# First group's x prepared during the last attention pair, decoded weights copied by ScalarE, x items spread over each group

## The chip, the cores and the metric

One core of a Trainium2 chip runs the whole program. The metric is the device time of one execution in microseconds (us). Engines: PE is TensorE's matmul, PEld its weight load, DVE VectorE, ACT ScalarE, POOL GpSimd, SP SyncE, which issues nearly all the DMAs here.

## The reference

Attention with queries pooled in pairs, then a gated dense layer, then a routed layer with eight experts. All in float32.

```python
q_pool = q.reshape(B, H, S // 2, 2, D).mean(axis=3)          # B, H, S, D = 4, 8, 1152, 64
scores = scale * np.matmul(q_pool, k.transpose(0, 1, 3, 2))
attn = softmax(scores); attn_out = np.matmul(attn, v)
x = attn_out.transpose(0, 2, 1, 3).reshape(2304, 512)
h = x @ w_in                                                 # d_ff = 2048
g = np.where(h >= 1, h, np.where(h <= -1, 0.0, (h + 1) ** 2 / 4))
x = g @ w_out
... # then each row goes through the expert that a softmax gate picks, with F = 1024
```

(The softmax is written out here in a word; the third stage is not touched by the change.)

## The kernel before

**Precision.** Each float32 operand of a matmul is split into a high part (`hi_part`, a copy that rounds) and a low part (a subtraction). A product is three matmuls: high by high, high by low, low by high.

**Attention** runs 16 pairs of heads, nine steps `s` to a pair, `nt` = 144 steps, and eight more (144 to 151) that drain it. A step on PE is six matmuls `sc` (nine where t = 4), nine transposes `pa`, `pb` of the step two before, and eight `av` matmuls. DVE then takes scores and their minimum out of PSUM into `e` (L235) and makes the low part `ptl` of the transposed probabilities (L271); ACT makes the exponential of `e` in place (L242) and the high part `pth` (L269); POOL splits the next pair's q, k and v. Each engine runs its instructions in the order in which the code issues them. There is one PSUM buffer for `sc` and one for `pa`. The raw q, k and v of a pair lie in the pool `prep`. `store` writes the result of a pair to DRAM (`av_b`, `av_t`), `sums` the reciprocals of the softmax sums (`rs_b`).

**The first group's x.** The dense layer takes its rows in four groups of 5, 5, 5 and 3 tiles of 128. x of a group is built from `av_b` and `rs_b`: `x_raw` loads the first half of the sum (`xth`) and the reciprocals, spread over partitions (`xtl`), `x_load` the second half; `x_item` adds and multiplies on POOL (L535, L536), and its `ev` makes the high part on ACT (L539) and the low part on DVE (L540). A group of five tiles has five such items: one for each quarter of the 512 columns for four tiles, and one for the fifth tile. The rows of group 0 need the heads of batches 0 and 1 alone, that is pairs 0 to 7. Its x tiles lie where `prep` lay, so they are loaded once `prep` is released, at step 141, and the items are issued in the steps from 144 on.

**The dense layer** has 16 steps `j` to a group. A step is two halves of 12 matmuls `h` (L563) with `h_act` behind each (ACT L578, L581, L584, DVE L582, and in group 0 POOL L586 for the low part `gl`), then 15 matmuls `y` (L595) of the step before. So `h` of step j + 1 stands on PE behind `y` of step j - 1. There are two PSUM buffers for `h`.

**The weights** come as 64-bit floats. `decode` makes float32 of one half of a step's weights (`wi` or `wo`) in three DVE operations (L449, L453, L457), called pieces; behind the third, POOL makes the high part `wh` (L57) and the low part `wl` (L461). The first three steps' weights (`EARLY`) are decoded during attention. The other 13 are decoded in group 0: 78 pieces, five in each step, called `fillers`: one behind ACT's first operation of a half, one behind DVE's L582, and one at the end of the step. Behind each third piece SP issues the load of the next step's raw half; there are two raw buffers (tag `m` of the pool `stage`) and two for the decoded words (tag `w`).

**Order.** Within group g, the raw x of group g + 1 is loaded at j = 1, 3, 5, 7, and the items are issued one a step from the end of step 9 to that of step 13, each `ev` a step later.

Of the kernel before, what the change touches and what calls it, by code (L numbers as in the profile page):

```python
# [20 lines left out]
NQ = S // 2  # L21
# [53 lines left out]
class Attention:  # L75
# [11 lines left out]
    def open(self, ctx):  # L87
# [5 lines left out]
        self.prep = tc.alloc_tile_pool(name="a_prep", bufs=1, side="right")  # L93
        self.ktp = pool("a_kt", 2)
# [47 lines left out]
    def load_v(self, n):  # L142
        b, hp = divmod(n, 4)
        d = self.st[n]
        d["vr"] = self.prep.tile([128, 18, 64], F32, name="vr")
# [175 lines left out]
    def run(self, aside, tail):  # L321
# [18 lines left out]
        for s in range(nt + 8):  # L340
# [39 lines left out]
            if s == nt - 3:  # L380
                self.prep.release()
                g.extend(tail())
            if self.post and self.post[0][0] < s:
                self.post.popleft()[1]()
            if s >= nt and g:
                for f in g.popleft():
                    f()
# [9 lines left out]
class Weights:  # L397


    def __init__(self, nc, w_in, w_out, stage, pools):  # L400
        self.nc, self.stage, self.pools = nc, stage, pools
        self.w_in, self.w_out = w_in.bitcast(U32), w_out.bitcast(U32)
        self.raw, self.t = {}, {}
# [20 lines left out]
    def pieces(self, j):  # L424
# [3 lines left out]
        def piece(i):  # L428
            if i == 0:
                box.extend(self.decode(j))  # L430
            box[i]()
            if i % 3 == 2 and j + 1 < NF:
                self.load(j + 1, i // 3)
        return [lambda i=i: piece(i) for i in range(6)]

    def decode(self, j):
# [6 lines left out]
        out = []  # L443
        for i in range(2):
# [11 lines left out]
            def third(i=i, box=box):  # L456
                nc.vector.scalar_tensor_tensor(out=box["w"], in0=raw[j, i][:, :, 0], scalar=29, in1=box["w"],  # L457
                                               op0=ALU.logical_shift_right, op1=ALU.bitwise_or)
                w = box["w"].bitcast(F32)
                hi_part(nc.gpsimd, hi[:, i], w, nc)  # L460
                nc.gpsimd.tensor_sub(out=lo[:, i], in0=w, in1=hi[:, i].bitcast(F32))  # L461
# [5 lines left out]
class Moe1:  # L467
# [26 lines left out]
    def x_raw(self, g, ks=None):  # L494

        hi, r = (a.bitcast(F32) for a in self.xt[g])
        for k in ks or [slice(0, 4)]:
            for c, n, b, o in self.ranges(g):
                self.nc.sync.dma_start(out=hi[:, k, c:c + n],
                                       in_=self.xs.av[b][k, 0, :, o:o + n].rearrange("k p c -> p k c"))  # L500
                for h in range(2):
                    src = [(c, n, b, h * (NQ + 64) + o)]
                    if b >= B:
                        src = [(c + 64 * i, 64, 2 * (b - B) + i, 512 + 64 * h) for i in range(2)]
                    for c1, n1, b1, o1 in src:
                        rs = self.xs.rs[b1][None, k, o1:o1 + n1]
                        self.nc.sync.dma_start(out=r[64 * h:64 * h + 64, k, c1:c1 + n1],
                                               in_=rs.to_broadcast([64, k.stop - k.start, n1]))
# [110 lines left out]
    def run(self, route, xt2, moe2):  # L619
# [3 lines left out]
        self.fillers.extend(p for j in range(EARLY, NF) for p in ws.pieces(j))  # L623
        for k in range(len(steps) + 1):
            self.flush()
            if k < len(steps):
# [19 lines left out]
                if g + 1 < ng and j in (1, 3, 5, 7):  # L646
# [872 lines left out]
```

## Time and profile before

| what | value |
|---|---|
| time, median of 3 runs | 1192.37 us (1190.85 to 1193.21) |
| the profiled execution | 1190.95 us, its span 1189.1 us |
| mean granted clock of TensorE | 0.987 |
| busy share of the span | PE 96%, PEld 90%, DVE 74%, ACT 62%, POOL 50% |

The span runs from the first to the last instruction; the 1.85 us between it and the execution's time lie around it. A clock of 1.00 is TensorE's higher level, 2.4 GHz, 0.50 its lower, 1.2 GHz. A share of busy time is an average over stages: attention ends at about 479 us, group 0 of the dense layer at about 624 us.

### The profile page before, as it was taken

The page shows a single profiled execution, that of the slowest core. Times are in us where ns is not written, and L with a number is a line of the kernel's source. Part 1 is how long each engine was busy: PE and PEld are TensorE (multiplying, and loading weights), DVE is VectorE, ACT ScalarE, POOL GpSimd, SP SyncE. Part 2 cuts the span into 40 slices and gives each one's busy share as a digit, 9 for nine tenths or more (in the row PEclk, how much of TensorE's full clock was granted, in tenths as well). Part 3 has the DMA queues.
Part 4 walks back from the last instruction along what each step waited for, and adds up shares of the span by engine and source line. Part 5 has one row for each costly group of instructions (what it writes and reads, how often), then busy time and mean ns, then how long its engine had stood idle before and what let it go on. Part 6 is the DMA issues. An engine that isn't in the chain of part 4 may idle for free. (4 is left out here: it accounts for less than half of the span.)

```text
span 1189.1 us, 21181 instructions
## 1 busy us (share of the span) xinstructions
PE 1145.3 (96%) x7315; PEld 1064.7 (90%) x7315; DVE 882.1 (74%) x1593; ACT 740.6 (62%) x1451; POOL 600.4 (50%) x525
## 2 busy tenths in 40 slices
PE   7999999999999999799789999999999999999997
PEld 6999999999999999689679988998889899887886
DVE  6888898899999998698845674565455776666775
ACT  5888888878788787344334445444435466666664
POOL 6998988877888872698950222012110221121211
PEclk9999999999999999899989999999999999999999
DMA  7787777785869754555314211111222121286443
GB/s 186 176 191 175 173 183 172 167 204 141 208 151 214 169 124 122 162 168 165 123 46 124 72 46 66 55 54 32 78 89 93 46 72 37 77 267 210 141 144 131
DMA packets 87189, 156.14 MB, mean 131 GB/s; under 512 B 26871, under 2 KB 44279, under 8 KB 87056
## 3 DMA queue, kind: packets, MB, share of 16 engines
q1 hardware_dynamic: 82352, 142.34, 44.7%
q0 software_dynamic: 4336, 11.58, 2.9%
q8 instruction: 67, 1.10, 0.4%
q10 hardware_dynamic: 368, 0.59, 0.2%
q14 instruction: 66, 0.54, 0.2%
HBM read 145.84 MB, written 20.08 MB: 140 GB/s over the span
## 5 line engine op out<-in xcount | busy, mean ns | idle before, releaser
L235 DVE TENSOR_SCALAR_CACHE_REDUCE e<-sc 128x1152 f32<-128x1152 f32 x144 | 194.7, 1352 | 23.5 <-PE sc L231 22.2
L242 ACT ACTIVATE e<-e,nm 128x1152 f32<-128x1152 f32 x144 | 183.7, 1276 | 4.8 <-DVE e L235 4.8
L231 PE MATMUL sc<-kT,qt 128*128 128x384 f32 x780 | 159.0, 339 | 9.8 <-DVE e L235 8.2
L269 ACT CAST pth<-pa 128x768 fp32r<-128x768 f32 (+2 forms) x160 | 116.3, 737 | 80.5 <-PE pa L260 80.5
L271 DVE TENSOR_TENSOR ptl<-pa,pth 128x768 fp32r<-128x768 f32 (+2 forms) x160 | 138.9, 876 | 19.9 <-ACT pth L269 7.7
L1173 DVE TENSOR_TENSOR e<-e,e 128x512 fp32r<-128x512 f32 x200 | 129.4, 687 | 30.2 <-ACT e L1172 14.2
L582 DVE SCALAR_TENSOR_TENSOR u<-h,u 128x320 f32<-128x320 f32 (+1 forms) x112 | 55.8, 498 | 128.8 <-ACT u L581 128.2
L578 ACT ACTIVATE u<-h,half 128x320 f32<-128x320 f32 (+1 forms) x112 | 59.8, 534 | 142.7 <-PE h L563 134.3
L231 PEld LDWEIGHTS sc<-kT,qt 128*128 128x128 f32 x780 | 132.2, 188 | 12.3 <-DVE e L235 9.6
L1269 PE MATMUL d_po<-e,e 128*128 128x512 f32 x504 | 120.9, 393 | 0.0
L260 PE MATMUL pa<-idf,e 128*128 128x128 f32 x864 | 117.6, 272 | 1.7 <-DVE ptl L271 1.7
L595 PE MATMUL y<-wh,gl 128*128 128x512 f32 x288 | 113.9, 395 | 0.8 <-POOL gl L586 0.8
L1172 ACT CAST e<-e 128x512 fp32r<-128x512 f32 x200 | 113.7, 619 | 0.7 <-issue 0.3
L595 PE MATMUL y<-wh,gh 128*128 128x512 f32 x288 | 113.9, 395 | 0.0
L595 PE MATMUL y<-wl,gh 128*128 128x512 f32 x288 | 113.6, 394 | 0.0
L1277 POOL DMA_INDIRECT out<-d_ob,d_rec x19 | 22.1, 1162 | 176.9 <-ACT d_ob L1276 120.5
L1269 PEld LDWEIGHTS d_po<-e,e 128*128 128x128 f32 x504 | 92.6, 188 | 18.6 <-DVE e L1173 0.3
L260 PEld LDWEIGHTS pa<-idf,e 128*128 128x128 f32 x864 | 102.9, 140 | 7.0 <-DVE ptl L271 1.3
L563 PE MATMUL h<-xth,wh 128*128 128x320 f32 (+1 forms) x448 | 90.8, 325 | 16.5 <-POOL wh L57 9.5
L584 ACT CAST gh<-u 128x320 fp32r<-128x320 f32 (+1 forms) x112 | 52.4, 468 | 84.9 <-DVE u L582 84.9
L535 POOL TENSOR_TENSOR xl<-xth,xl 128x512 f32<-128x512 f32 (+1 forms) x14 | 18.3, 1306 | 168.6 <-DMA xl<-av_b 139.9
L285 PE MATMUL av<-pth,vh 128*128 128x288 f32 x576 | 103.2, 306 | 0.0
(257 smaller groups left out, 2639.0 us busy)
## 6 DMA issues: line engine op xcount, KB each, us to landing
e<-moe_w SPq DMA_DIRECT2D x104, 512.0 KB
kr<-k SPq DMA_DIRECT2D x63, 288.0 KB
qr<-q SPq DMA_DIRECT2D x62, 288.0 KB
kk<-kT SPq DMA_DIRECT2D x60, 288.0 KB
vr<-v SPq DMA_DIRECT2D x16, 576.0 KB
av_b<-avs SPq DMA_DIRECT2D x64, 128.0 KB
wi<-moe_w_in SPq DMA_DIRECT2D x16, 512.0 KB
wo<-moe_w_out SPq DMA_DIRECT2D x16, 512.0 KB
```

The lines of the kernel that those rows point to most:

```text
L231: nc.tensor.matmul(s[:, j, 0:384], lhsT=a, rhs=b[:, 384 * j:384 * j + 384], start=i == 0, stop=i == len(mm) - 1)
L235: nc.vector.tensor_scalar(out=e.rearrange("p (a b) -> p a b", a=3), in0=s[:, :, 0:384], scalar1=-0.5 / D ** 0.5, scalar2=None, op0=ALU.mul ...
L242: self.nc.scalar.activation(e, e, AF.Exp, bias=d["nm"][:, t:t + 1], scale=-1.0, accum_out=d["sum"][:, t:t + 1])
L260: nc.tensor.transpose(p[:, c // 3, (c % 3) * 128:(c % 3) * 128 + 128], e[:, i * 128:(i + 1) * 128], idf)
L269: nc.scalar.copy(hi, p)
L271: nc.vector.tensor_sub(out=lo, in0=p, in1=hi.bitcast(F32))
L285: nc.tensor.matmul(box["t"][:, 0:GQ], lhsT=self.vh[:, h * 9 + i % 9], rhs=p[:, i % 9, c0:c0 + GQ], start=i == 0, stop=i == 17)
L563: nc.tensor.matmul(ps[:, :n], lhsT=a[:, k], rhs=b[:, k, h0:h0 + n], start=i == 0, stop=i == 11)
L595: self.nc.tensor.matmul(y, lhsT=a, rhs=b, start=j == 0 and q == 0, stop=j == NF - 1 and q == 2)
L1172: self.nc.scalar.copy(hi, r)
L1173: self.nc.vector.tensor_sub(out=lo, in0=r, in1=hi.bitcast(F32))
L1269: self.nc.tensor.matmul(self.o, lhsT=(self.hh, self.hl)[a][f // 4][:, f % 4, s], rhs=self.w[b, f // 2][:, f % 2], start=f == 0 and q == 0, ...
```

## The change

- The raw v of a pair gets a pool of its own, and `prep` is released at step 135 in place of 141. The loads of group 0's x go out there, 22 in place of 37, in the order in which the items use them. The items are issued in steps 139 to 143, each `ev` one step later.
- The load of step 3's raw weights is issued at step 146 in place of 147.
- For steps 3 to 15 the high part of a decoded half is made by ACT in place of POOL, and this copy and POOL's subtraction are issued behind the next piece in place of the third. Steps 4 and 9 take one piece more.
- In each group the raw x of the next is loaded by parts at j = 1, 4, 7, 10, 12, the second halves from j = 2, and the items are issued at the end of steps 5, 8, 11, 13 and 14.

```diff
--- before.py
+++ after.py
@@ -91,6 +91,7 @@
         self.prep = tc.alloc_tile_pool(name="a_prep", bufs=1, side="right")
+        self.vp = pool("a_v", 1)
...
     def load_v(self, n):
...
-        d["vr"] = self.prep.tile([128, 18, 64], F32, name="vr")
+        d["vr"] = self.vp.tile([128, 18, 64], F32, name="vr")
...
-            if s == nt - 3:
+            if s == nt - 9:
                 self.prep.release()
                 g.extend(tail())
             if self.post and self.post[0][0] < s:
                 self.post.popleft()[1]()
-            if s >= nt and g:
+            if s >= nt - 5 and g:
                 for f in g.popleft():
                     f()
...
@@ -428,7 +429,10 @@
         def piece(i):
             if i == 0:
                 box.extend(self.decode(j))
+            late, self.late = self.late, []
             box[i]()
+            for f in late:
+                f()
             if i % 3 == 2 and j + 1 < NF:
                 self.load(j + 1, i // 3)
...
+        def split(i, w, e):
+            hi_part(e, hi[:, i], w, nc)
+            nc.gpsimd.tensor_sub(out=lo[:, i], in0=w, in1=hi[:, i].bitcast(F32))
...
-                w = box["w"].bitcast(F32)
-                hi_part(nc.gpsimd, hi[:, i], w, nc)
-                nc.gpsimd.tensor_sub(out=lo[:, i], in0=w, in1=hi[:, i].bitcast(F32))
+                if j < EARLY:
+                    split(i, box["w"].bitcast(F32), nc.gpsimd)
+                else:
+                    self.late.append(lambda: split(i, box["w"].bitcast(F32), nc.scalar))
...
-    def x_raw(self, g, ks=None):
+    def x_raw(self, g, i):
...
-        for k in ks or [slice(0, 4)]:
-            for c, n, b, o in self.ranges(g):
-                self.nc.sync.dma_start(out=hi[:, k, c:c + n],
...
+        ks, c0, c1 = self.parts(g)[i]
+        for c, n, b, o in self.ranges(g):
+            a, e = max(c, c0), min(c + n, c1)
+            if a >= e:
+                continue
+            self.nc.sync.dma_start(out=hi[:, ks, a:e],
+                                   in_=self.xs.av[b][ks, 0, :, o + a - c:o + e - c].rearrange("k p c -> p k c"))
...
@@ -621,6 +635,7 @@
         self.fillers.extend(p for j in range(EARLY, NF) for p in ws.pieces(j))
+        self.fillers.append(lambda: [f() for f in ws.late])
...
-                if g + 1 < ng and j in (1, 3, 5, 7):
-                    self.x_raw(g + 1, [slice(j // 2, j // 2 + 1)])
-                if g + 1 < ng and j == 8:
+                if g + 1 < ng and j in (1, 4, 7, 10, 12) and j // 3 < len(self.parts(g + 1)):
+                    self.x_raw(g + 1, j // 3)
+                if g + 1 < ng and j == 2:
                     load(0)
                     load(1)
-                if g + 1 < ng and j == 9:
-                    self.xprep.extend(nxt)
+                if g + 1 < ng and j in (5, 8, 11, 13, 14) and nxt:
+                    self.xprep.append(nxt.pop(0))
...
                 if g == 0:
-                    self.fill(5 - 2 * len(halves))
+                    self.fill(5 - 2 * len(halves) + (j in (4, 9)))
...
@@ -1437,17 +1452,16 @@
-                if s == last:
-                    for i in range(5):
-                        m1.x_load(0, i, ws.rows(i, 5))
-                if s == last + 12:
+                if s == last + 11:
                     ws.load(EARLY)
...
-                m1.x_raw(0, [slice(k, k + 1) for k in range(4)])
+                for i in range(5):
+                    m1.x_raw(0, i)
+                    m1.x_load(0, i, ws.rows(i, 5))
```

The order of instructions on DVE in the last steps of attention and behind them, before: the low parts of the last steps' probabilities, the sums, then all five `xtl`, and the first decode piece.

```order
L271 TENSOR_TENSOR ptl_117<-pa_6210,pth_116 128x6x128
L271 TENSOR_TENSOR ptl_117<-pb_6211,pth_116 128x3x128
L271 TENSOR_TENSOR ptl_117<-pa_6246,pth_116 128x6x128
L271 TENSOR_TENSOR ptl_117<-pb_6247,pth_116 128x3x128
L305 RECIPROCAL r_125<-r_125 128x9
L306 STREAM_TRANSPOSE rt_6261<-r_125 128x32
L540 TENSOR_TENSOR xtl_6105<-rows_5868,xth_6104 128x512 x2
L540 TENSOR_TENSOR xtl_6105<-rows_5871,xth_6104 128x512 x2
L540 TENSOR_TENSOR xtl_6105<-row_5874,xth_6104 128x4x128
L449 TENSOR_SCALAR wf_6384<-wi_6311 128x512
```

The same engine with the change, in steps 140 to 142 (line numbers are those of the changed file).

```order
L236 TENSOR_SCALAR e_6064,nm_5834<-sc_6057 128x1152
L272 TENSOR_TENSOR ptl_120<-pa_6066,pth_119 128x6x128
L272 TENSOR_TENSOR ptl_120<-pb_6067,pth_119 128x3x128
L554 TENSOR_TENSOR xtl_5876<-rows_5880,xth_5875 128x512
L236 TENSOR_SCALAR e_6106,nm_5834<-sc_6099 128x1152
L272 TENSOR_TENSOR ptl_120<-pa_6108,pth_119 128x6x128
L272 TENSOR_TENSOR ptl_120<-pb_6109,pth_119 128x3x128
L554 TENSOR_TENSOR xtl_5876<-rows_5880,xth_5875 128x512
L236 TENSOR_SCALAR e_6143,nm_5834<-sc_6136 128x1152
```

An `xtl` now stands between the low parts of one step and the `e` of the next, in steps 140 to 143. On ACT the `xth` that it reads stands behind the exponential of the same step.

The order on POOL at the end of group 0, before: steps 12 and 13 of the dense layer (`wh13` is the high part of step 13's weights).

```order
L586 TENSOR_TENSOR gl_7251<-u_7252,gh_7250 128x320
L57 TENSOR_SCALAR wh13_7254<-wf_7256 128x512
L461 TENSOR_TENSOR wl13_7255<-wf_7256,wh13_7254 128x512
L586 TENSOR_TENSOR gl_7251<-u_7276,gh_7250 128x320
L535 TENSOR_TENSOR xl_7228<-xth_6363,xl_7228 128x512
L536 TENSOR_TENSOR xl_7228<-xl_7228,xtl_6364 128x512
L57 TENSOR_SCALAR wh13_7254<-wf_7285 128x512
L461 TENSOR_TENSOR wl13_7255<-wf_7285,wh13_7254 128x512
L586 TENSOR_TENSOR gl_7325<-u_7326,gh_7324 128x320
L57 TENSOR_SCALAR wh14_7335<-wf_7337 128x512
L461 TENSOR_TENSOR wl14_7336<-wf_7337,wh14_7335 128x512
```

The same engine with the change, from the second half of step 12 to the items of step 14.

```order
L600 TENSOR_TENSOR gl_7236<-u_7263,gh_7235 128x320
L451 TENSOR_TENSOR wl13_7194<-wf_7244,wh13_7193 128x512
L600 TENSOR_TENSOR gl_7312<-u_7313,gh_7311 128x320
L451 TENSOR_TENSOR wl14_7293<-wf_7294,wh14_7292 128x512
L600 TENSOR_TENSOR gl_7312<-u_7336,gh_7311 128x320
L549 TENSOR_TENSOR xl_7066<-xth_6352,xl_7066 128x512
L550 TENSOR_TENSOR xl_7066<-xl_7066,xtl_6353 128x512
L451 TENSOR_TENSOR wl14_7293<-wf_7338,wh14_7292 128x512
L600 TENSOR_TENSOR gl_7381<-u_7382,gh_7380 128x320
L451 TENSOR_TENSOR wl15_7385<-wf_7386,wh15_7384 128x512
L600 TENSOR_TENSOR gl_7381<-u_7408,gh_7380 128x320
L549 TENSOR_TENSOR xl_7290<-xth_6352,xl_7290 128x512
```

The `wh` copies are gone from POOL, and no item stands behind step 12. The 26 copies now stand on ACT: in `h_act` between its operations, or at the end of a step.

## Rows read from the trace of the kernel before

**Rows 1.** The page, part 1: busy time, share of the span, instructions.
```profile
PE 1145.3 (96%) x7315; PEld 1064.7 (90%) x7315; DVE 882.1 (74%) x1593; ACT 740.6 (62%) x1451; POOL 600.4 (50%) x525
```
**Rows 2.** Busy time by stretch (us): length, then engines, TensorE's clock, DMA share, GB/s.
```profile
479.00:496.65 17.65, 10.66 (x50) 9.16 (x48) 8.79 (x12) 5.88 (x12) 8.56 (x9) 0.81 0.50 147
496.65:560.20 63.55, 63.28 (x354) 57.01 (x352) 56.54 (x66) 25.45 (x54) 56.44 (x50) 1.00 0.57 178
560.20:620.59 60.39, 49.81 (x236) 43.34 (x235) 40.35 (x45) 20.03 (x41) 49.69 (x42) 0.89 0.29 92
620.59:683.60 63.01, 63.01 (x353) 56.99 (x352) 37.67 (x98) 30.48 (x67) 7.28 (x5) 1.00 0.31 93
```
**Rows 3.** Waits from 494 to 612 us: total, times, longest.
```profile
PE h L563 <- POOL wh L57: 9.5, 4, 3.1
```
**Rows 4.** POOL's groups from 494 to 612 us: busy, mean ns, idle before.
```profile
L461 POOL TENSOR_TENSOR wl<-wf,wh 128x512 fp32r<-128x512 f32 x25 | 36.2, 1448 | 2.1
L586 POOL TENSOR_TENSOR gl<-u,gh 128x320 fp32r<-128x320 f32 x29 | 36.0, 1247 | 0.1
L57 POOL TENSOR_SCALAR wh<-wf 128x512 fp32r<-128x512 f32 x25 | 19.6, 782 | 7.7 <-DVE wf L457 7.7
L535 POOL TENSOR_TENSOR xl<-xth,xl 128x512 f32<-128x512 f32 x5 | 7.5, 1504 | 0.0
L536 POOL TENSOR_TENSOR xl<-xl,xtl 128x512 f32<-128x512 f32 x5 | 6.9, 1384 | 0.4
```
**Rows 5.** Groups of DVE, and one of ACT, in the same stretch.
```profile
L453 DVE SCALAR_TENSOR_TENSOR wf<-wo,wf 128x512 uint32<-128x512 uint32 x12 | 16.7, 1389 | 0.2
...
L457 DVE SCALAR_TENSOR_TENSOR wf<-wi,wf 128x512 uint32<-128x512 uint32 x13 | 16.1, 1238 | 0.2
...
L582 DVE SCALAR_TENSOR_TENSOR u<-h,u 128x320 f32<-128x320 f32 x29 | 14.0, 484 | 12.2 <-ACT u L581 11.6 <-POOL wh L57 0.5
L449 DVE TENSOR_SCALAR wf<-wo 128x512 uint32<-128x512 uint32 x13 | 10.0, 768 | 2.3 <-POOL wl L461 1.5 <-DMA wo<-moe_w_out 0.7
...
L539 ACT CAST xth<-xl 128x512 fp32r<-128x512 f32 x5 | 3.1, 616 | 0.7 <-POOL xl L536 0.7
```
**Rows 6.** Timeline: start, length, instruction, [idle before]; steps 140 and 141 of attention.
```profile
459.57 1.36 DVE L235 TENSOR_SCALAR_CACHE_REDUCE e<-sc 128x1152 f32<-128x1152 f32 x1 [0.19 <-PE sc L231]
...
461.29 1.27 ACT L242 ACTIVATE e<-e,nm 128x1152 f32<-128x1152 f32 x1
...
462.66 1.36 DVE L235 TENSOR_SCALAR_CACHE_REDUCE e<-sc 128x1152 f32<-128x1152 f32 x1 [0.18 <-PE sc L231]
```
**Rows 7.** Timeline of DVE: two of the five low parts of group 0's x.
```profile
484.73 1.09 DVE L540 TENSOR_TENSOR xtl<-rows,xth 128x512 fp32r<-128x512 f32 x1 [3.80 <-DMA rs_b<-rt]
487.65 0.69 DVE L540 TENSOR_TENSOR xtl<-row,xth 128x512 fp32r<-128x512 f32 x1 [1.83 <-ACT xth L539]
```
**Rows 8.** Timeline of PE from attention's end to the first y.
```profile
477.70 1.35 PE L285 MATMUL av<-ptl,vh 128*128 128x288 f32 x9
...
484.75 0.64 PE L563 MATMUL h<-xth,wh 128*128 128x320 f32 x1 [4.28 <-DMA rs_b<-rt]
...
485.19 1.33 PE L563 MATMUL h<-xtl,wh 128*128 128x320 f32 x4
...
492.39 0.86 PE L563 MATMUL h<-xth,wh 128*128 128x320 f32 x4 [1.53 <-DVE u L582]
...
496.65 0.39 PE L595 MATMUL y<-wh,gh 128*128 128x512 f32 x1
```
**Rows 9.** Timeline of DVE, and of SP's queue, around the first raw weights.
```profile
477.97 0.21 DVE L306 STREAM_TRANSPOSE rt<-r 128x32 f32<-128x32 f32 x1
...
483.05 1.51 SPq L309 DMA_DIRECT2D rs_b<-rt  x4
...
487.14 0.54 SPq L417 DMA_DIRECT2D wi<-moe_w_in  x1
...
491.51 0.43 DVE L449 TENSOR_SCALAR wf<-wi 128x512 uint32<-128x512 uint32 x1 [3.17 <-DMA wi<-moe_w_in]
```

More of the change, by code (lines that the diff above doesn't have):

```diff
@@ L402, in __init__ @@
         self.w_in, self.w_out = w_in.bitcast(U32), w_out.bitcast(U32)
-        self.raw, self.t = {}, {}
+        self.raw, self.t, self.late = {}, {}, []
     def rows(self, i, n):
@@ L492, in ranges @@
         return out
-    def x_raw(self, g, ks=None):
+    def x_raw(self, g, i):
         hi, r = (a.bitcast(F32) for a in self.xt[g])
-        for k in ks or [slice(0, 4)]:
-            for c, n, b, o in self.ranges(g):
-                self.nc.sync.dma_start(out=hi[:, k, c:c + n],
[L500 to L508, printed above, removed]
+        ks, c0, c1 = self.parts(g)[i]
[5 more added lines that the diff above has]
+                                   in_=self.xs.av[b][ks, 0, :, o + a - c:o + e - c].rearrange("k p c -> p k c"))
+            for h in range(2):
+                if b < B:
+                    src = [(a, e, b, h * (NQ + 64) + o + a - c)]
+                else:
+                    src = [(c + 64 * t, c + 64 * t + 64, 2 * (b - B) + t, 512 + 64 * h) for t in range(2)]
+                for a1, e1, b1, o1 in src:
+                    rs = self.xs.rs[b1][None, ks, o1:o1 + e1 - a1]
+                    self.nc.sync.dma_start(out=r[64 * h:64 * h + 64, ks, a1:e1],
+                                           in_=rs.to_broadcast([64, ks.stop - ks.start, e1 - a1]))
     def parts(self, g):
```

## The prediction

> **What bounds the kernel now.** I read the page's busy shares first, then busy time and clock by stretch, then the waits and groups of the stretch that loses most, and last the timelines at its two ends. PE is busy for 96% of the span [rows 1], so only PE's idle time and its time at the lower clock can be won. The stretches show where these lie [rows 2]. From 620.59 to 683.60 us, nine steps of group 1 (from one first `y` to the ninth after it), PE has no idle time at clock 1.00: a step needs 63.01 / 9 = 7.00 us. Group 0 has the same work. Its first nine steps, from 496.65 to 560.20, take 63.55, 0.5 more. The next six, from 560.20 to 620.59, take 60.39 in place of 42.0: 18.4 lost, 10.6 of them as idle time and the rest at clock 0.50 (mean 0.89). Ahead of group 0, from 479.00 to 496.65, PE is busy for 10.7 of 17.65 us at a mean clock of 0.81.
>
> What ends the wait in the bad stretch is POOL: `h` waits 9.5 us in four waits for `wh` [rows 3]. POOL is not idle there: 49.69 of 60.39 us [rows 2]. Its groups [rows 4] give its work per step: two `wh` at 0.78, two `wl` at 1.45, two `gl` at 1.25, 6.95 us, just under PE's 7.00. An item of x adds 1.50 + 1.38 = 2.89. Before, five items stand in five successive steps, 9.84 us each, so POOL falls behind by up to 5 × 2.84 = 14.2 us, and `wh`, which PE needs, stands in that queue.
>
> **The change, part by part.**
>
> *Group 0.* The 26 copies leave POOL: 5.39 us a step, 8.28 in a step with an item. Behind steps 5, 8 and 11 the next steps leave 1.6 us each and clear the 1.28 of excess; only 13 and 14 stand together, 2.6 us behind at most. The weights' `wl` that is tightest is that of step 15, issued in the second half of step 14: behind the item of step 13 I count it ending some 4.8 us after that half's matmuls, and `h` of step 15 wants it after 3.5 us of `y` and two thirds of the first 1.76 us of `h`, at 4.7. So it is about even, and I leave 0.5 us for it. On ACT a copy of 128x512 takes 0.62 [rows 5]; 26 are 16 us, and ACT is busy for 45.5 of these 124 us [rows 2], so they lie in its idle time. A copy waits for a word that DVE finished one piece before, ahead of the `u` that ACT's half waits for in any case. I leave 1 us more for what I can't see. Of 0.5 + 18.4 = 18.9 that makes a gain of **17.4**; bounds 9 (rival 1) and 18.9.
>
> *The last steps of attention.* This was free before: `xth` and `xtl` ran behind the last scores. Now they stand in steps 140 to 143, in line. In a step before, `e` follows PE's scores by 0.19 us of waiting, the pace being 462.66 - 459.57 = 3.09, PE's [rows 6]. With the change a loop through two engines closes: `e` 1.36, the exponential behind it at 461.29 and 1.27 long, `xth` 0.62 [rows 5], then `xtl`, then the next `e`. From 459.57 to the exponential's end is 2.99; with `xth` 3.61; `xtl` takes 0.69 alone and 1.09 beside a POOL operation [rows 7], so 4.3 to 4.7, and some 0.15 of handing over. The pace goes from 3.09 to about 4.6. Three such steps (the `e` of 141, 142 and 143) are late by **4.5** in sum; the `xtl` of 143 and 144 have no scores behind them. Bounds 3.6 (0.69 each) and 6 (the drain delayed too, and a lower clock there).
>
> The Trainium skill ("SBUF — State Buffer", section "SBUF: two separate sides") has VectorE and GpSimd take their shared ports as an exclusive lock for a whole instruction. By that an `xtl` behind a POOL addition of some 1.3 us would take up to 2.0, and the three steps would lose 2.7 us more; the rows show 1.09, and the sum goes by them.
>
> *Between attention and the first `y`.* Before, PE has its last `av` block at 477.70, waits 4.28 until 484.75 for x, then 1.53 until 492.39 for DVE's `u`, which stands behind the first decode piece, which waits for the raw weights [rows 8, 9]. The first wait goes: all of x is ready when the drain ends. The second does not. Its chain starts at the sums: `rt` ends at 478.18, SP would then issue four `rs_b` and four stores and only then `wi`. SP was late with 37 loads and began `rs_b` at 483.05, `wi` at 487.14, landed at 491.51 [rows 9]. With the change SP is free, but `rt` is 4.5 later: 482.7, `wi` at 482.7 + 4.1 = 486.8, landed 4.4 later at 491.2, 0.3 earlier than before. So all that the freed SP gives is taken by attention's delay. PE meanwhile has done both halves of step 0 (3.5 us from about 483.4) and stands from about 486.9 to 492: some 5 us idle in one piece, where 4.28 before was followed by a lower clock (four matmuls in 1.33 at 485.19) [rows 8]. In 479.00 to 496.65 a mean of 0.81 is 6.7 us at 0.50 [rows 2], which cost little before, since PE had to wait for the weights all the same. Now it would fall on the halves behind the wait. I take 0.3 won, 2.3 lost by the clock (between nothing and the half of 6.7): **a loss of 2.0**, bounds 5 lost (the drain at the lower clock too, `rt` later by it) and 1 won (no lower clock, `xtl` at 0.69). The 4.5 us are in this, not beside it. The load one step earlier changes nothing, as SP reaches it behind the sums.
>
> *The 22 loads.* They go out at about 444, ahead of `rs_b` and the stores of pair 14, which nobody waits for soon. I cost them at nothing: POOL has no x to wait for before about 450, and the DMAs that were spread until 483 are done by 460.
>
> *Groups 1 to 3.* PE is full there [rows 2]. The last item of groups 0 and 1 comes two steps later than before, its `xtl` at about the moment that PE wants it. I take **0.4 lost** in sum, between nothing and 2.
>
> Sum: 17.4 - 2.0 - 0.4 = 15.0. The profiled execution took 1190.95, so 1176.0. It is 1.4 below the median of the three runs, 1192.37; for a median I say **1177**.
>
> **The rivals.**
>
> 1. *VectorE becomes the bound of group 0.* By its groups [rows 5] a step costs six pieces, 2 × (0.77 + 1.39 + 1.24), and two `u` at 0.48: 7.76, more than 7.00, and 1.1 more with an `xtl`. For it: these are means of the very stretch. Against: in the nine steps to 560.20 DVE is busy for 56.54 of 63.55, 6.2 a step, and PE still full [rows 2], and POOL, beside which DVE is slow, has less to do now. If it holds, 0.6 to 0.7 a step over 15 steps are lost and 9 are won: 1190.95 - 9 + 2.4 = 1184.4, as a median 1186.
>
> 2. *Slower: the copies stretch ACT's and DVE's chain.* A `wh` copy stands between ACT's two operations on `u`, and DVE's L582, behind which all later pieces stand, waits for the second. L582's group waits 11.6 us for ACT now [rows 5]. If every copy's 0.62 went onto that chain, in both halves, a step would be 7.76 + 1.24 = 9.0, and 15 steps 135: 11 more than the 123.9 now, with the 2.4 ahead and behind 1204.5, as a median 1206. It decides from 8.1 a step, where the gain of group 0 only pays for these 2.4. Against: a copy is issued a piece late just so that its word is ready, and DVE has a piece to do while it runs.
>
> 3. *Nothing is won because POOL stays late.* `wl` takes the place of `wh` in the same queue and PE waits for it in the second third of `h`. Then the four waits move by one operation and the stretch keeps some 15 of its 18.9: 1190 to 1192. Against: 6.8 us a step on the mean of steps 5 to 14 is less than 7.00.
>
> 4. *More is won*: no lower clock ahead of group 0, short `xtl`, nothing lost in group 0: 18.9 + 1 = 19.9, 1171 as a profile, 1172.5 as a median.
>
> **How the numbers follow.** The forecast, 1173 to 1182 as a median, gets 0.72, rival 1 0.14, rival 2 0.05, rival 3 0.04, rival 4 0.05. The range from 1171 to 1186 holds the forecast, rival 4 and most of rival 1: a little over 8 in 10. Runs of this kernel spread by 0.2%, 2.4 us, about what a measurement can tell from no change. Faster by more than that: forecast, rivals 1 and 4, 0.91. Within it: most of rival 3, 0.03. Slower: rival 2 and the rest, 0.06.
>
> **What would show it.** Right: from the first to the last `y` block of group 0 some 106.5 us where it was 123.9, PE's waits there for `wh` or `wl` together under 2 us, POOL busy for about 5.4 to 6.5 of each 7.0. The `e` operations of steps 141 to 143 about 4.6 us apart, with DVE waiting for ACT's `xth`; `wi` issued at about 487; one idle piece of PE of some 5 us behind the first two halves of `h`, ended by DVE's `u`, and a clock of 0.50 behind it; the first `y` at 497 to 499. Wrong: a first `y` ahead of 495 or behind 502; DVE without idle time in group 0 and PE waiting for `u` or decoded words (rival 1); PE waiting for `wl` (rival 3); waits of over 1 us in each step that end in ACT's copies (rival 2).

## The result

The changed kernel takes 1179.97 us (median of 4 runs, 1178.18 to 1183.04), 1192.19 before (4 runs). The ratio is 0.991, 95% interval 0.9893 to 0.9927: 12 us faster. The profiled execution took 1178.18 us, its span is 1176.4, the mean clock 0.995.

Part 1 of the changed kernel's page, to set beside [rows 1]:

```profile
PE 1135.4 (97%) x7315; PEld 1056.2 (90%) x7315; DVE 883.1 (75%) x1593; ACT 753.2 (64%) x1477; POOL 580.7 (49%) x499
```

PE is busy for 10 us less with as many instructions: it is at the lower clock for less of the time (mean clock 0.995, before 0.987). Its busy time by stretch (columns as in [rows 2]): attention's end, the first nine steps of group 0, its next six, and nine steps of group 1.

```profile
479.00:497.38 18.38, 13.29 (x85) 13.02 (x83) 8.60 (x14) 6.32 (x14) 3.44 (x3) 0.81 0.41 126
497.38:560.91 63.53, 63.30 (x353) 57.11 (x352) 55.00 (x65) 33.34 (x69) 47.11 (x37) 1.00 0.50 159
560.91:608.03 47.12, 43.68 (x236) 37.87 (x235) 39.05 (x45) 24.48 (x51) 37.09 (x29) 1.00 0.44 134
608.03:671.05 63.02, 63.02 (x353) 56.99 (x352) 40.41 (x99) 30.98 (x68) 10.17 (x7) 1.00 0.26 80
```

The six steps that took 60.39 us take 47.12, at clock 1.00, with POOL busy for 37.09 where it was 49.69 [rows 2]. Six steps of 7.00 are 42.0, so 5.1 are left there; with the 0.5 of the first nine steps 5.6.

The waits of 493 to 612 us in which group 0 still loses (total, times, longest):

```profile
DVE wf L458 <- POOL wl L451: 3.6, 2, 2.4
DVE wf L458 <- DMA wi<-moe_w_in: 2.7, 3, 1.4
...
PE h L577 <- DVE u L596: 1.7, 2, 1.4
...
PE h L577 <- ACT wh L59: 1.5, 2, 1.2
```

`wh` is no longer awaited from POOL [rows 3]; `u` and ACT's copies end what little waiting is left on PE, and DVE waits for POOL's `wl` and for raw weights.

The timeline of the changed kernel's attention steps 140 to 142, and of the way to the first `y`:

```profile
460.68 1.36 DVE L236 TENSOR_SCALAR_CACHE_REDUCE e<-sc 128x1152 f32<-128x1152 f32 x1 [0.18 <-PE sc L232]
...
463.65 0.62 ACT L553 CAST xth<-rows 128x512 fp32r<-128x512 f32 x1
...
464.30 0.73 DVE L554 TENSOR_TENSOR xtl<-rows,xth 128x512 fp32r<-128x512 f32 x1 [0.71 <-ACT xth L553]
...
464.96 1.34 DVE L236 TENSOR_SCALAR_CACHE_REDUCE e<-sc 128x1152 f32<-128x1152 f32 x1
...
466.36 1.31 PE L232 MATMUL sc<-kT,qt 128*128 128x384 f32 x6 [0.58 <-DVE e L236]
...
467.51 1.28 POOL L549 TENSOR_TENSOR rows<-xth,rows 128x512 f32<-128x512 f32 x1
...
468.29 1.05 DVE L554 TENSOR_TENSOR xtl<-rows,xth 128x512 fp32r<-128x512 f32 x1 [0.65 <-ACT xth L553]
...
469.26 1.35 DVE L236 TENSOR_SCALAR_CACHE_REDUCE e<-sc 128x1152 f32<-128x1152 f32 x1
...
482.39 0.21 DVE L307 STREAM_TRANSPOSE rt<-r 128x32 f32<-128x32 f32 x1
...
486.54 0.55 SPq L418 DMA_DIRECT2D wi<-moe_w_in  x1
...
491.21 0.43 DVE L458 TENSOR_SCALAR wf<-wi 128x512 uint32<-128x512 uint32 x1 [8.62 <-DMA wi<-moe_w_in]
...
492.09 1.43 PE L577 MATMUL h<-xth,wh 128*128 128x320 f32 x4 [5.09 <-DVE u L596]
...
497.38 0.39 PE L609 MATMUL y<-wh,gh 128*128 128x512 f32 x1
```

The `e` operations are 4.28 and 4.30 apart where they were 3.09 [rows 6]: exponential, `xth`, `xtl`, next `e`, without a gap in DVE ahead of the `e`, and PE waits for it. `rt` comes 4.4 later than before, `wi` is issued at 486.54 where it was 487.14 [rows 9], and PE stands for 5.09 us. Four matmuls take 1.43 behind that, 0.74 ahead of it: the granted clock is 1.00 from 483 to 487 us and 0.50 from 489 to 495.

### The profile page after: what moved, and what is told of

The parts are those of the page before. It is cut to its first block, busy times and chain, and to the rows that moved or that the text cites. A ratio compares the mean times of both kernels' runs of the same rounds, so it can differ in the third digit from the quotient of the medians.

```text
span 1176.4 us, 21181 instructions
## 1 busy us (share of the span) xinstructions
PE 1135.4 (97%) x7315; PEld 1056.2 (90%) x7315; DVE 883.1 (75%) x1593; ACT 753.2 (64%) x1477; POOL 580.7 (49%) x499
## 3 DMA queue, kind: packets, MB, share of 16 engines
HBM read 145.84 MB, written 20.08 MB: 141 GB/s over the span
## 5 line engine op out<-in xcount | busy, mean ns | idle before, releaser
L286 PE MATMUL av<-ptl,vh 128*128 128x288 f32 x576 | 102.2, 304 | 0.0
L577 PE MATMUL h<-xth,wh 128*128 128x320 f32 (+1 forms) x448 | 87.8, 318 | 8.3 <-DVE u L596 6.8
```

The source lines that it names most:

```text
L286: nc.tensor.matmul(box["t"][:, 0:GQ], lhsT=self.vh[:, h * 9 + i % 9], rhs=p[:, i % 9, c0:c0 + GQ], start=i == 0, stop=i == 17)
L577: nc.tensor.matmul(ps[:, :n], lhsT=a[:, k], rhs=b[:, k, h0:h0 + n], start=i == 0, stop=i == 11)
```

## The experiments

Executions drift by some us against each other before they come to the changed steps. So three distances are compared: **front**, from `e` of step 140 (460.68 in the changed kernel, 459.57 before) to the first `y` of group 0; **group 0**, from there to the start of its sixteenth step's first `y`; **rest**, from there to the span's end. Each is from one profiled execution; medians and ratios (to the kernel before on the same chip, 95% interval) are from all runs. The chips differ from row to row; the kernel before takes 1190.65 to 1192.19 on them, so two rows are compared by their ratios where it is close.

| kernel | front | group 0 | rest | median | ratio |
|---|---|---|---|---|---|
| before | 37.08 | 123.94 | 568.5 | 1192.19 | 1 |
| changed | 36.70 | 110.65 | 568.3 | 1179.97 | 0.991 [0.9893, 0.9927] |
| e1_front | 36.60 | 122.69 | 571.7 | 1194.85 | 1.0035 [1.002, 1.0051] |
| e2_group0 | 34.34 | 109.89 | 569.7 | 1175.07 | 0.9863 [0.9843, 0.9884] |
| e3_copies | 34.76 | 114.40 | 570.7 | 1180.13 | 0.9903 [0.9884, 0.9922] |
| e4_spread | 32.74 | 123.42 | 569.7 | 1190.75 | 1.0 [0.9986, 1.0013] |
| e5_drain | 34.40 | 111.07 | 569.6 | 1176.69 | 0.9883 [0.9858, 0.9909] |
| e6_load | 30.46 | 110.52 | 569.5 | 1175.97 | 0.9873 [0.9849, 0.9897] |
| e8_at_once | 36.29 | 118.79 | 568.1 | 1189.00 | 0.9987 [0.997, 1.0003] |
| e10_no_items | 38.16 | 105.36 | 572.7 | 1182.74 | 0.9939 [0.9919, 0.996] |
| e9_both | 27.36 | 111.60 | 566.4 | 1168.96 | 0.982 [0.98, 0.9839] |
| e11_behind | 36.47 | 109.57 | 573.3 | 1179.99 | 0.9901 [0.9885, 0.9917] |
| e13_lead | 27.35 | 111.90 | 570.8 | 1171.30 | 0.9828 [0.9811, 0.9845] |
| e14_early | 27.36 | 115.32 | 571.5 | 1175.10 | 0.9863 [0.9838, 0.9889] |

The rest differs by up to 7 us between executions. Of it, the way to the last block of `y` of group 3 takes 300.2 us in every row, so the differences lie behind it, in the routed layer, which no edit touches (e10_no_items changes what it works on). So the first two columns tell where time goes, and the median tells what an edit is worth.

### The change in its parts

**e1_front**: the attention part alone; copies on POOL, items and their loads as before.

```diff
-                    self.late.append(lambda: split(i, box["w"].bitcast(F32), nc.scalar))
+                    split(i, box["w"].bitcast(F32), nc.gpsimd)
...
-                if g + 1 < ng and j in (5, 8, 11, 13, 14) and nxt:
-                    self.xprep.append(nxt.pop(0))
+                if g + 1 < ng and j == 9:
+                    self.xprep.extend(nxt)
```

> The change's part in attention alone (x of group 0 prepared in the last pair, raw weights one step earlier); in group 0 POOL makes the high parts and the items stand as before. My theory, that the raw weights' wait takes the place of the wait for x: no gain, 1190 to 1194 us, first y at 497 to 498.5 us, from first to last y of group 0 about 124 us. Rival, that the earlier x is worth something by itself: 1188 us or less, first y at 494 or earlier.

Measured: front 36.60, about that of before, and the time 0.35% longer. Alone it wins nothing. The 4 us that it loses on the median don't lie in front or group 0, which are shorter than before. In the profiled execution 1.5 us lie ahead of step 140 and 3.1 behind group 3, in stages that the edit doesn't touch; why is not shown.

**e2_group0**: the dense-layer parts alone; x of group 0 is loaded at step 141 and made behind attention as before, but with 27 loads in place of 37.

```diff
-            if s == nt - 9:
+            if s == nt - 3:
...
-            if s >= nt - 5 and g:
+            if s >= nt and g:
...
-                if s == last + 11:
+                if s == last:
+                    for i in range(5):
+                        m1.x_load(0, i, ws.rows(i, 5))
+                if s == last + 12:
                     ws.load(EARLY)
```

> The change's parts in the dense layer alone (copies on ACT a piece later, one piece more in steps 4 and 9, items spread); group 0's x is prepared behind attention as before (27 loads in place of 37). My theory, that the whole gain is made here: 1178 to 1181 us, as the full change or 1 us less, first y at 496 to 497.5, group 0 about 110.7 us from first to last y. Rival, that the parts need each other: 1184 or more.

Measured: 1175.07, 4.9 us under the whole change and 3 under the expected range; the intervals of the two ratios don't meet. Group 0 is 0.8 under what was expected, and the first `y`, at 493.59, comes 2.4 earlier than expected at the earliest. The timeline of SP's queue and PE:

```profile
481.86 0.55 SPq L418 DMA_DIRECT2D wi<-moe_w_in  x1
...
487.41 1.43 PE L577 MATMUL h<-xth,wh 128*128 128x320 f32 x4 [3.33 <-DVE u L596]
```

With ten loads fewer SP is free when the sums come: `rs_b` goes out at 477.89, right behind `rt`, where it was 483.05 [rows 9], `wi` at 481.86 in place of the changed kernel's 486.54, with no work moved into attention, and PE's wait is 3.33. So the loads' number was what made SP late before, and moving x into attention undid this gain.

**e3_copies** is e2_group0 with the items where they were before (j == 9, one a step); **e4_spread** is e2_group0 with the copies on POOL, issued at once. The edits are those of e1_front, one each.

> As the one before, with the items of x unspread (steps 9 to 13 again). POOL then has 5.39 us a step and 8.28 in five successive ones, 6.4 us behind at their end. My theory, that both parts count: group 0 about 115 to 118 us, 1184 to 1187 us. Rival, that the copies alone carry the gain: 1178 to 1181 us.

> The items spread, but POOL makes the high parts as before, at once, five pieces in each step. POOL has 6.95 us in a plain step and 9.84 in five of the ten from 5 to 14, and no step that clears the excess. My theory: spreading alone wins little, group 0 about 121 to 124 us, 1189 to 1193 us. Rival, that it was the crowding of the items: 1184 us or less.

Measured: the copies alone bring group 0 from 123.94 to 114.40, the spread alone to 123.42, both to 109.89. With `wh` on POOL spreading is worth nothing; once it is gone, 4.5. "The copies alone" are all of e3_copies: ACT in place of POOL, a piece later, and the two steps of six pieces. Its group 0 is 0.6 under what the theory had, but its time, 1180.13, lies in the rival's range and not in the theory's 1184 to 1187, in part as the expectation had not counted the 2.3 us that the front wins by fewer loads. Copies that stay on POOL and are issued a piece later were not tried. e4_spread came out as expected.

### The front

**e5_drain**: `xth` and `xtl` behind the last `e`, two parts in a step.

```diff
-                return [[lambda i=i: one(i) if i < 5 else None, lambda i=i: evs[i - 1]() if i else None]
-                        for i in range(6)]
+                evp = {4: (0, 1), 5: (2, 3), 6: (4,)}
+                return [[lambda i=i: one(i) if i < 5 else None] + [lambda k=k: evs[k]() for k in evp.get(i, ())]
+                        for i in range(7)]
```

> The five parts of x are rounded and subtracted (xth, xtl) from step 143 on, behind its last e, two parts each in the steps 143 and 144 and one in 145; their additions and products on POOL stay where they are. Theory (the loop e, exponential, xth, xtl, e costs the 4.3 us pace): the e operations of 141 to 143 go back to some 3.1 us apart, rt ends 3.6 us earlier, at about 478.8, SP issues wi at about 483 and the first y comes at some 493.8 in place of 497.4; the time is 3.5 us under that of the changed kernel, 1176 to 1177. Rival (the loop's loss is hidden behind x or the weights, as other waits end later): the pace goes back but the first y stays at 496.5 to 497.5 and the time within 1 us of the changed kernel, since five xth and xtl in a row end later than the drain and PE then waits for x.

**e6_load**: the first raw weights' load two steps earlier.

```diff
-                if s == last + 11:
+                if s == last + 9:
                     ws.load(EARLY)
```

> The load of the first raw weight tile of the dense layer is issued two steps earlier, in step 144, ahead of the four sums and four stores on SP that wait for rt. Theory (the second wait ahead of the first y is that of SP's order): wi is issued before 481 and landed before 486, PE's 5.09 us idle piece behind the first two halves of h goes, with it the low clock behind it, and the first y comes at 490.5 to 491.5; the time is 6 to 6.5 us under that of the changed kernel, 1173 to 1175. Rival (DVE, not the load, is late there, or the load competes with the sums): PE still waits 3 us or more for u, and the time is less than 2.5 us under the changed kernel.

Timeline of e5_drain: two `e`, then SP, DVE, POOL and PE ahead of the first `y`.

```profile
463.38 1.36 DVE L236 TENSOR_SCALAR_CACHE_REDUCE e<-sc 128x1152 f32<-128x1152 f32 x1 [0.18 <-PE sc L232]
...
466.47 1.36 DVE L236 TENSOR_SCALAR_CACHE_REDUCE e<-sc 128x1152 f32<-128x1152 f32 x1 [0.18 <-PE sc L232]
...
483.02 0.54 SPq L418 DMA_DIRECT2D wi<-moe_w_in  x1
...
487.74 0.43 DVE L458 TENSOR_SCALAR wf<-wi 128x512 uint32<-128x512 uint32 x1 [7.98 <-DMA wi<-moe_w_in]
...
488.49 0.68 DVE L462 SCALAR_TENSOR_TENSOR wf<-wi,wf 128x512 uint32<-128x512 uint32 x1
...
488.62 1.43 PE L577 MATMUL h<-xth,wh 128*128 128x320 f32 x4 [5.16 <-DVE u L596]
...
491.29 1.28 POOL L451 TENSOR_TENSOR wl<-wf,wh 128x512 fp32r<-128x512 f32 x1 [1.28 <-ACT wh L59]
491.33 1.79 DVE L462 SCALAR_TENSOR_TENSOR wf<-wo,wf 128x512 uint32<-128x512 uint32 x1
```

The pace is 3.09 again and `wi` goes out 3.5 us earlier, 3.1 counted from step 140. The front shrinks by 2.3, 1.3 less than the theory's 3.6, and the time by 3.3, as expected. Of the 1.3, 0.5 is missing at `rt` already. The other 0.8 lies behind the landing: PE's idle piece is as long as before (5.16), and the clock of 0.50 lasts until 494.0, for 5.4 us of PE's work where it was 3.7 in the changed kernel. That x would be awaited (the rival) is not seen.

The same stretch of e6_load:

```profile
470.89 0.40 SPq L418 DMA_DIRECT2D wi<-moe_w_in  x1
...
484.05 0.38 DVE L458 TENSOR_SCALAR wf<-wi 128x512 uint32<-128x512 uint32 x1
...
490.80 0.86 PE L577 MATMUL h<-xth,wh 128*128 128x320 f32 x4 [0.37 <-DVE u L596]
```

The load goes out 13 us ahead of DVE's use, and PE's 5.09 us shrink to 0.37 at full clock. The front is 6.2 shorter, as expected; the median 4.0 less, where 6 to 6.5 were expected.

By the medians alone neither edit is clear of noise: the intervals of both ratios overlap the changed kernel's by a little. The fronts, and the next run, decide.

**e9_both** has both edits.

> Both edits ahead of the first y together: xth and xtl behind the last e, and the first raw weight tile loaded in step 144 ahead of the sums and stores. Theory (the loop and SP's order are two losses that add): the loop's 3.6 us and the idle piece of 5.1 us with its low clock both go, the first y comes at about 488 (497.4 less 3.5 and less 6.2, with up to 1.5 us of drift between executions ahead of the changed steps), and the time is 8 to 10 us under that of the changed kernel, 1170 to 1172. Rival (x is the next wait: with five xth and xtl in a row, the last of them ends behind the drain): PE waits 1.5 us or more for xtl or xth ahead of the first h and the time is 1173 to 1175, as with the load alone.

PE in e9_both, the first `h` and the first `y`:

```profile
478.91 0.74 PE L577 MATMUL h<-xth,wh 128*128 128x320 f32 x4
...
486.75 0.39 PE L609 MATMUL y<-wh,gh 128*128 128x512 f32 x1
```

Front 27.36, 9.3 under the changed kernel's, where 2.3 and 6.2 are 8.5: the two losses add. It is the fastest of all, 1168.96, 1 us under the expected range, and its ratio, 0.982 [0.98, 0.9839], is clear of the changed kernel's.

### Group 0

**e8_at_once**: copy and subtraction right behind the third piece.

```diff
-                    self.late.append(lambda: split(i, box["w"].bitcast(F32), nc.scalar))
+                    split(i, box["w"].bitcast(F32), nc.scalar)
```

> ACT's copy and POOL's subtraction of a decoded piece are issued right behind the third operation on its word, not a piece later; everything else is as in the changed kernel. Theory (the piece later pays, as ACT does not wait for a word that DVE has yet to finish; but it also keeps each of the two word buffers a piece longer): from the first to the last y of group 0 it is slower, 111.5 to 114 in place of 110.65, PE's waits for DVE's u grow, and the time is 1 to 4 us over that of the changed kernel. Rival (the remaining 5.6 us of group 0 come from the word buffers that are held longer): DVE's waits for POOL's wl fall under 1 us in sum, the stretch takes 108 to 109.5 and the time is 1 to 2.5 us under that of the changed kernel.

The waits of e8_at_once, 493 to 612 us:

```profile
ACT wh L59 <- DVE wf L466: 48.1, 26, 3.1
...
DVE u L596 <- ACT u L595: 21.0, 21, 1.4
...
PE h L577 <- DVE u L596: 4.7, 6, 1.3
```

Group 0 takes 118.79 and the time 9 us longer, more than twice what was expected at most. ACT waits 48.1 us at its copies for DVE's word (17.3 in the changed kernel); its second operation on `u` stands behind the copy, and DVE waits for that (21.0 us; 7.2 in the changed kernel). The rival fell: holding the word a piece longer is the cheaper.

**e10_no_items**: no items in group 0.

```diff
-                if g + 1 < ng and j in (5, 8, 11, 13, 14) and nxt:
+                if 0 < g < ng - 1 and j in (5, 8, 11, 13, 14) and nxt:
```

> The five items that prepare x of group 1 (POOL's addition and product, ACT's rounding, DVE's subtraction, and three of their five loads) are left out, so group 1 computes with unprepared values. Theory (the 5.6 us that group 0 still takes over 15 steps of 7.00 come from the items: in POOL's queue ahead of wl, beside DVE's operations and on DVE itself): from the first to the last y of group 0 105.1 to 106.5 in place of 110.65, no waits of DVE for wl, and the time 4 to 6 us under that of the changed kernel. Rival (DVE's chain of decoding bounds the steps by itself): at most 2 us of the 5.6 go, DVE stays busy for over 9 of 10 us behind step 10, and the time is 0 to 2 us under.

Group 0 takes 105.36, 0.3 over 15 steps of 7.00. From the first to the fifteenth `y` (98.35 us; 103.63 in the changed kernel) PE is busy throughout:

```profile
500.12:598.47 98.35, 98.35 (x548) 88.76 (x547) 84.55 (x102) 52.07 (x109) 64.51 (x53) 1.00 0.51 160
```

The whole time says nothing here: group 1 computes with other values, the routing sends rows elsewhere, and the execution reads 149.77 MB in place of 145.84. Its front is 1.5 longer, with a mean clock of 0.74 to 0.83 at 476 to 484 us, where the changed kernel's is 1.00. DVE's groups from the first to the fifteenth `y` (busy us, mean ns, idle before), of this kernel and then of the changed one:

```profile
L596 DVE SCALAR_TENSOR_TENSOR u<-h,u 128x320 f32<-128x320 f32 x29 | 14.1, 486 | 10.6 <-ACT u L595 10.3
...
L458 DVE TENSOR_SCALAR wf<-wi 128x512 uint32<-128x512 uint32 x12 | 7.9, 660 | 1.7 <-DMA wi<-moe_w_in 1.7
```

```profile
L596 DVE SCALAR_TENSOR_TENSOR u<-h,u 128x320 f32<-128x320 f32 x28 | 13.5, 482 | 4.5 <-ACT u L595 4.1
...
L458 DVE TENSOR_SCALAR wf<-wi 128x512 uint32<-128x512 uint32 x12 | 10.0, 835 | 5.3 <-DMA wi<-moe_w_in 2.7 <-POOL wl L451 2.4
...
L554 DVE TENSOR_TENSOR xtl<-xl,xth 128x512 fp32r<-128x512 f32 x4 | 5.2, 1307 | 0.6 <-ACT xth L553 0.6
```

Without items DVE waits 10.3 us for ACT's `u`: that is its slack, 0.7 a step. With them 4.1 are left. Four `xtl` take 5.2 and wait 0.6, and on `wi` L458 is 2.1 longer in sum and waits 3.6 more. In all DVE is busy for 90.71 us, 6.2 more than the 84.55 above. My reading is that PE loses what the slack of single steps does not hold. The changed kernel's PE is idle for 3.7 us in this stretch: 1.7 end with `u`, 1.5 with ACT's copies, 0.3 with POOL's `wl`, and the longest wait for a copy leads back to DVE's word:

```profile
596.38 0.62 ACT L59 CAST wh<-wf 128x512 fp32r<-128x512 f32 x1 [1.61 <-DVE wf L466]
...
597.05 0.85 PE L577 MATMUL h<-xth,wh 128*128 128x320 f32 x4 [1.23 <-ACT wh L59]
```

That the items cost 5.3 us is shown; that they do so on DVE is read from these rows, as the run takes their parts on POOL and ACT away too.

**e11_behind**: items in group 0 behind the pieces of their step. Two of five move behind a `wl`.

```diff
-                if self.xprep:
+                if self.xprep and g:
                     self.xevs.append(self.xprep.popleft()())
...
                     self.fill(5 - 2 * len(halves) + (j in (4, 9)))
+                    if self.xprep:
+                        self.xevs.append(self.xprep.popleft()())
```

> In group 0 POOL's addition and product of an item of x are issued at the end of a step behind its pieces, not ahead of them. On POOL this moves the items of two steps, the second and the fourth, behind a wl that they stood ahead of. Theory (of the 5.3 us that the items cost in group 0, the first 2 to 4 are the word buffer that a wl behind an item holds back, and the raw load that then starts late): the waits of DVE for POOL's wl go, the two stretched steps at 553 and 561 us (7.5 and 8.76) shrink by 1.5 to 2.3 together, from the first to the last y 108.3 to 109.2 in place of 110.65, and the time is 1.5 to 2.5 us under the changed kernel's. Rival (the loss is all DVE's own work, slow beside POOL's two-input operations, and only its place changes): 110 to 111.5 from the first to the last y and the time within 1 us of the changed kernel's.

The wait that it is to take away, in the timeline of the changed kernel:

```profile
552.78 1.74 POOL L549 TENSOR_TENSOR xl<-xth,xl 128x512 f32<-128x512 f32 x1
...
556.20 1.28 POOL L451 TENSOR_TENSOR wl<-wf,wh 128x512 fp32r<-128x512 f32 x1
...
557.51 1.09 DVE L458 TENSOR_SCALAR wf<-wi 128x512 uint32<-128x512 uint32 x1 [2.44 <-POOL wl L451]
...
562.20 0.38 SPq L418 DMA_DIRECT2D wi<-moe_w_in  x1
...
566.35 1.00 DVE L458 TENSOR_SCALAR wf<-wi 128x512 uint32<-128x512 uint32 x1 [1.41 <-DMA wi<-moe_w_in]
...
567.80 0.85 PE L577 MATMUL h<-xth,wh 128*128 128x320 f32 x4 [1.43 <-DVE u L596]
```

An item at 552.78 delays `wl`, which holds a word buffer; DVE waits 2.44. The third piece is late by it, and by an `xtl` ahead of it; so is the raw load behind it (562.20), and 4 us later DVE waits again, and PE 1.43. With e11_behind the waits for `wl` are gone and the step at 553 is 7.00 (7.50 before), but the raw weights are still awaited:

```profile
564.07 0.90 DVE L458 TENSOR_SCALAR wf<-wi 128x512 uint32<-128x512 uint32 x1 [1.53 <-DMA wi<-moe_w_in]
```

Group 0 takes 109.57, 1.1 less, under the 1.5 to 2.3 expected, and the median is the same. The buffer is a fifth of the 5.3 at most; the time does not show it.

**e13_lead** (e9_both with a sixth piece in steps 1, 3, 5 and 9 in place of 4 and 9) and **e14_early** (e9_both, e11_behind's edit, items issued in steps 3, 5, 7, 9, 11, the sixth piece in 12 and 13) try to have decoded weights in hand when the items come.

```diff
-                    self.fill(5 - 2 * len(halves) + (j in (4, 9)))
+                    self.fill(5 - 2 * len(halves) + (j in (1, 3, 5, 9)))
```

> As e9_both, and in group 0 the sixth piece of a step is issued in steps 1, 3, 5 and 9 in place of 4 and 9, so that decoding is ahead by one to two pieces when the items come. Theory (a step of five pieces with an item is just over 7.00 us on DVE, so the loss falls where the lead in decoded weights is used up): from the first to the last y 107 to 109 in place of 110.65, and the time 1.5 to 3.5 us under e9_both's. Rival (the lead can't be had, as the raw weights' two buffers and their load time hold DVE back): DVE's waits for raw weights grow to over 4 us in sum and the stretch takes 110 to 112.

Waits of e13_lead in its group 0:

```profile
DVE wf L458 <- DMA wi<-moe_w_in: 4.6, 5, 1.8
...
DVE wf L458 <- POOL wl L451: 2.4, 1, 2.4
...
DVE wf L458 <- DMA wo<-moe_w_out: 2.0, 3, 1.0
```

These are 6.6 us of waiting for raw weights. The rival's sign, over 4 us, was set against the changed kernel's 2.7 and 0.5; e9_both, from which this run differs in the pieces alone, has 2.7 and 1.6 already. So the growth is 2.3. Group 0 takes 111.90, e9_both 111.60, and the median is 2.3 more with overlapping intervals: nothing is won, as the rival said, and raw weights are part of the reason.

```diff
-                if g + 1 < ng and j in (5, 8, 11, 13, 14) and nxt:
+                if g + 1 < ng and j in ((5, 8, 11, 13, 14) if g else (3, 5, 7, 9, 11)) and nxt:
...
-                    self.fill(5 - 2 * len(halves) + (j in (4, 9)))
+                    self.fill(5 - 2 * len(halves) + (j in (12, 13)))
```

> e9_both, and in group 0 the five items of group 1's x stand two or three steps earlier (issued in steps 3, 5, 7, 9 and 11 in place of 5, 8, 11, 13 and 14, behind the pieces of their step, their loads moved with them), the two steps of six pieces are 12 and 13 in place of 4 and 9. Theory (an item costs nothing while decoded weights are in hand: the first item of the changed kernel, in step 5, cost nothing, and the loss falls in the last seven steps, where the lead of three decoded weights is used up): from the first to the last y of group 0 106 to 108.5 in place of e9_both's 111.6, and the time 3 to 5.5 us under e9_both's 1168.96, at 1163.5 to 1166. Rival (DVE's queue is in order, so a late operation there delays u and with it PE at any step, lead or not): the stretched steps only move forward, the stretch stays at 110 to 112 and the time at 1168 to 1170.

It is 6 us slower than e9_both, group 0 at 115.32. Two of PE's waits in the first half of the stretch:

```profile
529.80 0.85 PE L577 MATMUL h<-xth,wh 128*128 128x320 f32 x4 [0.39 <-DVE u L596]
...
545.25 0.85 PE L577 MATMUL h<-xth,wh 128*128 128x320 f32 x4 [0.82 <-DVE u L596]
```

It is `u` that PE waits for here, not weights; later it waits for ACT's copies too, 3.1 us in four waits. The theory fell: moved ahead, the items still cost. That `u` stands in the same queue of DVE, lead or not, fits the two waits; but DVE also waits 5.0 us for raw `wo`, so how much of a lead there was is open. The loss is worse than the rival's 110 to 112; which of the four moves in this kernel made it so was not taken apart. Nor is it settled why the first item of the changed kernel, in step 5, costs nothing.

## Why the prediction held, step by step

The three distances explain the profiled 12.8 us: group 0 gives 13.3, the front 0.4, the rest 0.2, and drift takes 1.1. The drift is there at step 134 (`e` at 440.48 before, 441.59 now), ahead of step 135, from which on x is loaded.

**Group 0: right in mechanism, 17.4 mis-sized, 13.3 measured.** The copies leaving POOL are the gain (e3_copies), and they cost nothing on ACT as long as they are issued a piece late (e8_at_once: 8.1 us otherwise). What failed is what it left for the rest, "I leave 0.5 us for it" (POOL's `wl`) and "I leave 1 us more for what I can't see": 5.6 are left. PE's waits for `wh` and `wl` are 1.8 us in sum, under 2 as predicted, and POOL was no longer the limit. e10_no_items shows that the items make all but 0.3 of the 5.6; DVE's rows put this on DVE's slack. POOL's count itself was too high: it has two `wh` and two `wl` in each step, 6.95 us, but five pieces are 1.67 words, and the rows of before have 56.44 / 9 = 6.27 [rows 2]. It erred on the safe side, as 5.39 with the change is by the same count 4.9. Rival 1 had the right engine and too high a price, 9.9 in place of 5.6, for the same reason: it charged six pieces to every step, 7.76 us; five are 5.66 + 0.97 = 6.6, under 7.00.

**The loop in attention: right, 4.5 mis-sized, 3.6 measured.** The pace is 4.28 to 4.30, the lower bound: the `xtl` took 0.73, 1.05 and 0.73, and the next `e` starts without the 0.15 of handing over. The 1.05 began at 468.29, 0.50 ahead of the end of POOL's addition at 467.51; the other two began 0.18 ahead of the end of a POOL operation. The rule of the Trainium skill that the prediction weighed ("SBUF — State Buffer", "SBUF: two separate sides") goes by which operation starts first; an estimate by it is 0.50 + 0.69 = 1.19 for the 1.05 and 0.18 + 0.69 = 0.87 for the 0.73, so the trace agrees within 0.14, and what did not occur is its worst case, 2.0.

**The front: right in its chain, -2.0 mis-sized, +0.4 measured.** `wi` at 486.8, landed at 491.2, PE idle for 5 us, the lower clock behind it, first `y` at 497 to 499: 486.54, 491.21, 5.09, 497.38. That the absolute times fit so well is luck in part: step 140 itself came 1.1 later in this execution. Against step 140 `rt` is 3.3 later than before where the prediction took 4.5, the landing 1.4 earlier (0.3 predicted), and from there to the first `y` it takes 1.0 longer (2.3 predicted). e6_load and e5_drain show the two causes, SP's order and the loop, and e9_both that they add. That the load one step earlier changes nothing was not tried alone; in the changed kernel's trace it still goes out behind the sums and four stores. Ahead of them it is worth 6.2 us of front and about 4 of the time.

**The loads: cost right, worth overlooked.** From `e` of step 134 to that of step 140, while the 22 loads go out, the kernel takes 19.09 us before and with the change. "All that the freed SP gives is taken by attention's delay" is what e2_group0 shows. But the prediction did not say that fewer loads alone, without moving x, would keep the gain: x was better made behind attention until the loop was taken apart (e9_both). e2_group0 with the early load of e6_load was not tried.

**Groups 1 to 3:** 0.4 lost predicted, nothing measured: from the sixteenth step of group 0 to the last of group 3 300.2 us, before and with the change. The 0.2 won in the rest lie behind them.

The errors have opposite signs (-4.1 in group 0, +2.4 in the front, +0.6 in the rest), and drift took 1.1 in this execution. So the mechanisms held, but that the 1176.0 of the prediction and the 1178.18 of the profile lie closer than the terms do is luck.

## What to carry to other kernels

Work that is moved into a loop of two engines costs, in every step, what the chain around the loop is then longer than the old pace, even where each engine has idle time: put it behind the last step that closes the loop, and issue a load that someone waits for ahead of transfers that nobody waits for. When work is taken off one engine, count the next engine's queue with its waits, not only its busy time; an in-order queue passes a late operand to everything behind it. Issuing a dependent copy one piece later, behind work that is ready, can be worth more than moving it to an idle engine: here 8.1 us of group 0 (e8_at_once to the changed kernel) against 4.6 (e4_spread to e8_at_once).

## What the runs showed of the hardware

The time of DVE's two-input operations on 128x512 depends on what POOL does. In e5_drain (above) L462 takes 0.68 with POOL idle nearly to its end, and 1.79 when it starts 0.04 behind a `wl` of 1.28. By the same section of the Trainium skill's page "SBUF — State Buffer", DVE's two-input operations and POOL's hold their shared ports for a whole instruction; an estimate by it is 1.24 + 0.68 = 1.92, so the trace agrees to 0.13. In the prediction I had taken the milder row.

TensorE's granted clock fell from 1.00 to 0.50 during each idle piece of 3.3 to 5.2 us shown here (e2_group0, e5_drain, the changed kernel) and stayed there for the first 3.7 to 5.7 us of work behind it, and it did not fall in e6_load and e9_both, where PE waited 0.37 between the first `h` and the first `y`. The length of the piece does not decide alone: behind one of 1.96 us in the drain the clock fell in e10_no_items (0.50 from 478 to 480 us) and stayed at 1.00 in e6_load and in the changed kernel, where PE stands for 1.96 us too.
